# Second-layer products two channels at a time at every other half slot, in chunks 3 to 6 of a memory-attention and mixer kernel

## The chip, the cores and the metric

The kernel runs on one core of a Trainium2 chip. TensorE (PE) multiplies out of SBUF into PSUM, ScalarE (ACT), VectorE (DVE) and GpSimd (POOL) do the rest, SyncE (SP) issues most DMAs, and ACT issues some. Each engine takes its instructions in the order in which the program lists them. The metric is the device time of the whole kernel in microseconds, median of several runs.

## The reference

Two parts follow each other. The first is an attention through a memory of 32 slots for each of 8 x 8 heads over 576 tokens; the second a mixer over tokens and then over channels:

```python
a = softmax(phi, axis=tokens);  k_m, v_m = a^T k, a^T v
x = softmax(scale * q k_m^T) v_m               # heads side by side: 8 x 576 x 512
u = x + (relu(x^T w_tok1) w_tok2)^T            # token mixer
out = u + relu(u w_ch1) w_ch2                  # channel mixer, 512 -> 1536 -> 512
```

All of it is float32. The kernel splits a float32 operand into a high and a low part and multiplies three times (high by high, high by low, low by high) where this matters.

## The kernel before

The channel mixer works on 9 chunks of 512 tokens. Chunks 0 to 2 are computed straight. Chunks 3 to 6 (class `Quarters`, from `WIN` = 3 to `DOUBLE` = 7) take the first layer by a scheme of seven products of quarters in place of eight; chunks 7 and 8 do this jointly (class `Double`). Beside the mixer of one chunk runs the attention of the batches that later chunks need, laid out by hand in half slots: `at(h, fn)` files a piece of attention work under a half slot, `run(h, ...)` issues it there.

The change lies in `quarters(c, p)`, one step of chunk c for one pair p of hidden pieces: 4 chunks of 6 steps, 24 steps. A step issues seven first-layer products, named 11, 21, T2, T1, T3, 22 and T4, each six matmuls of 256 columns (L335). They go to two PSUM banks, `a` (rows "qa") and `b` (rows "qb"): 11, T2, T3 and T4 to a; 21, T1 and 22 to b. A product that adds onto its bank (T2, T3, 22, T4) or writes it anew (T1) has to wait until the result before it has been read out of that bank, most often by an ACT copy, `out`, L2166. The next step's two products take the same two banks.

Between the products stands the second layer: `mix` takes from `todo` one output channel block of one hidden piece of the step before and issues its three matmuls of 512 columns into an accumulator bank (L197, `Chunk.second`). `todo` holds eight such triples in a step (two hidden pieces by four channel blocks), and in the first step of chunk 3 four. `point(x)` stands behind each product, and once more at the end: first the attention work of that half slot, then a triple. The attention work on PE is `step_s` and `step_kv` (L754, L655), `step_A` (L896), `step_R` (L915) and `step_u` (L936). On ACT and DVE it is a softmax (`S_max`, `S_sub`, `S_exp` on L776), casts (`a_pair` on L826, `v_pair` on L840) and copies out of the attention's own two PSUM banks.

`load_unit` on ACT's queue fetches the weights of the products three units ahead.

Of the kernel before, what the change touches and what calls it, by code (L numbers as in the profile page):

```python
# [27 lines left out]
def kernel(  # L28
# [109 lines left out]
    def relu_high(h, ps):  # L138
        nc.scalar.activation(out=h, in_=ps, func=AF.Relu)  # L139

    def relu_low(h, l, ps):
        nc.vector.scalar_tensor_tensor(  # L142
            out=l, in0=ps, scalar=0.0, in1=f32(h), op0=ALU.max, op1=ALU.subtract
        )
# [423 lines left out]
    def load_unit(n, eng=nc.scalar):  # L568
        m = n - 2 * NF * (DOUBLE - WIN + 1)
        if m >= 7 * NF // 4:  # L570
            return
        p, j = n // 4 % (NF // 2), n % 4
        t = sb.tile([P, 1024], F32R, tag="c1", name=f"unit{n}", bufs=NF)
        if m >= 0:
            units[n] = t.rearrange("p (o x m) -> p o x m", o=2, x=2)
            eng.dma_start(out=f32(t), in_=Sums2.to[:, m // (NF // 4), m % (NF // 4)])
            return
        units[n] = t.rearrange("p (o x a n) -> p o x a n", o=2, x=2, a=2)
        m = 512 if j == 3 else 1024
        nc.scalar.dma_start(out=f32(t)[:, :m], in_=sums[p].to[:, j, :m])  # L580
# [1516 lines left out]
    for p in range(NF // 2):  # L2097
        x, h = Sums2(p), 2 * NF * (WIN + min(p, 4)) + (8.5 if not p else (3.5, 1.5, 9.5)[max(p - 3, 0)])
# [23 lines left out]
    def run(h, *ks):  # L2122
        for k in ks:
            for fn, x in events.pop((h, k), ()):
                out = fn(*x)
                if callable(out):
                    out()
# [20 lines left out]
    def quarters(c, p):  # L2148
        ch, h, n = chunks[c], 2 * NF * c + 4 * p, 4 * ((c - WIN) * NF // 2 + p)
        todo = [(x, f, a) for x, f in before if f < x.end for a in range(NKK)]  # L2150
        before[:] = [(ch, 2 * p), (ch, 2 * p + 1)]
        (eh, el), (oh, ol) = ch.pieces(p)
        t0, t1 = slice(0, HW), slice(HW, CW)

        def mix(n=1):
            for x, f, a in todo[:n]:
                x.ch2(f, [a])
                if f == x.end - 1:
                    x.add(a)
            del todo[:n]  # L2160

        def tile(x):
            return pch.tile([P, CW], F32, tag="ch", name=f"{x}{p}" + ch.n, bufs=2)

        def out(to, ps):
            nc.scalar.copy(out=to, in_=ps[:, :HW])  # L2166

        def add(to, x, y):
            nc.vector.tensor_tensor(out=to, in0=x, in1=y, op=ALU.add)  # L2169

        def product(ps, k, name, first):
            if not k % 2:
                load_unit(n + k // 2 + AHEAD)
            ch.product(ps, units[n + k // 2][:, k % 2], name, first, name in ("21", "22", "T4"))

        if not whole:
            whole.append(sb.tile([P, 2, CW], F32, tag="c1", name="whole", bufs=NF))
        et, ot = whole[0][:, 0], whole[0][:, 1]

        def split_relu(h, l, x):  # L2180
            relu_high(h, x)
            relu_low(h, l, x)

        def point(x):
            run(h + x, -1, 0, 1)
            mix()

        a = tile("qa")
        product(a, 0, "11", True)
        out(et[:, t0], a)  # L2190
        point(0)
        b = tile("qb")
        product(b, 1, "21", True)
        out(ot[:, t0], b)
        add(et[:, t0], et[:, t0], ot[:, t0])
        point(0.5)
        product(a, 2, "T2", False)
        out(et[:, t1], a)
        split_relu(eh[:, t0], el[:, t0], et[:, t0])
        point(1)  # L2200
        product(b, 3, "T1", True)
        out(ot[:, t0], b)
        point(1.5)
        product(a, 4, "T3", False)
        out(ot[:, t1], a)
        add(ot[:, t1], ot[:, t0], ot[:, t1])
        point(2)
        product(b, 5, "22", False)
        add(et[:, t1], b[:, :HW], et[:, t1])
        split_relu(oh[:, t1], ol[:, t1], ot[:, t1])  # L2210
        point(2.5)
        product(a, 6, "T4", False)
        split_relu(eh[:, t1], el[:, t1], et[:, t1])
        split_relu(oh[:, t0], ol[:, t0], a[:, :HW])
        point(3)
        point(3.5)
# [203 lines left out]
```

## Time and profile before

| | us |
|---|---|
| median of 3 runs | 745.86 (745.27 to 747.5) |
| profiled execution, its own time | 745.9 |
| its span | 743.9 |
| PE busy | 735.6 (99%) |
| DVE busy | 494.4 (66%) |
| ACT busy | 343.5 (46%) |
| chunks 3 to 6, first to last product of L335 | 299.9 to 619 |

A busy PE in this profile is one whose matmuls overlap: a matmul's row is longer than the distance to the next one's start. In timelines it is therefore the starts that tell how fast PE goes. Where a start comes later than the distance of its neighbours would have it, PE waited. ACT, DVE and POOL rows have a measured end, start plus duration.

### The profile page before, as it was taken

Reading aid. Unit: us, or ns where it says so; the run is one execution under the profiler, and the core shown is the slowest. Engines: PE = TensorE matmul, PEld = TensorE weight load, DVE = VectorE, ACT = ScalarE, POOL = GpSimd, SP = SyncE. Lnnn points to the kernel's source line nnn. Section 1 sums busy time; section 2 is a strip of 40 time slices with the busy share of each in tenths; the row PEclk is TensorE's granted clock in tenths of the full one; section 3 lists DMA queues with packets and bytes.
Section 4 is the critical chain, followed back from the end, with each engine's and each line's share of the span. In section 5 each row is a group of like instructions: output and inputs, shape, how many; then the busy total and the mean of one; then the engine's idle time right before and its main releaser. Section 6 shows DMA issues by size and latency. Waiting matters only on the chain.

```text
span 743.9 us, 12846 instructions
## 1 busy us (share of the span) xinstructions
PE 735.6 (99%) x4889; PEld 627.1 (84%) x4889; DVE 494.4 (66%) x896; ACT 343.5 (46%) x742; POOL 71.7 (10%) x71
## 2 busy tenths in 40 slices
PE   8999999999999999999999999999999999999998
PEld 8678787787878888889898889888898998888887
DVE  4989873776657657767586738674766554655874
ACT  5789753242314243545363536363544553434431
POOL 1021014001122020110010101010101000000000
PEclk9999999999999999999999999999999999999999
DMA  8975530575924654869687877879567645676762
GB/s 345 415 255 159 217 106 1 148 246 157 280 60 124 204 151 126 283 208 316 198 236 284 242 265 221 292 218 319 171 203 239 213 141 180 255 252 207 273 216 86
DMA packets 98813, 158.33 MB, mean 213 GB/s; under 512 B 42208, under 2 KB 65632, under 8 KB 94304
## 3 DMA queue, kind: packets, MB, share of 16 engines
q1 hardware_dynamic: 80320, 98.92, 41.0%
q10 hardware_dynamic: 18432, 58.60, 23.8%
q8 instruction: 39, 0.64, 0.4%
q14 instruction: 22, 0.18, 0.1%
HBM read 121.57 MB, written 35.91 MB: 212 GB/s over the span
## 4 chain that ended last, share of the span: by engine, by line
PE 80%; DMA 6%; DVE 6%; SPq 3%; ACT 2%; POOL 1%; issue 1%; ACTq 0%; POOLq 0%; DVEq 0%
PE acc L197 24%; PE cp L174 10%; PE qa L335 7%; PE e L455 7%; PE u L936 6%; PE qb L335 5%; PE da L400 4%; PE db L400 3%; PE Ap L896 2%; DMA sums<-v 2%; SPq L716 1%; PE sp L754 1%; POOL a L827 1%; DMA kv<-in_kv_dram 1%; PE u L1618 1%; PE end L455 1%
## 5 line engine op out<-in xcount | busy, mean ns | idle before, releaser
L197 PE MATMUL acc<-qhh,c 128*128 128x512 f32 x256 | 98.9, 396 | 0.0
L197 PE MATMUL acc<-hh,c 128*128 128x512 f32 x288 | 96.6, 394 | 0.0
L335 PEld LDWEIGHTS qa<-xT,unit 128*128 128x128 f32 x432 | 60.7, 188 | 8.2 <-ACT whole L2166 2.3
L335 PEld LDWEIGHTS qb<-x,unit 128*128 128x128 f32 x432 | 60.9, 188 | 6.7 <-ACT whole L2166 0.6
L197 PEld LDWEIGHTS acc<-hh,c 128*128 128x128 f32 x288 | 54.1, 188 | 14.3 <-issue 3.2
L335 PE MATMUL qa<-xT,unit 128*128 128x256 f32 x432 | 63.1, 282 | 0.8 <-ACT whole L2166 0.8
L335 PE MATMUL qb<-x,unit 128*128 128x256 f32 x432 | 63.0, 281 | 0.0
L827 POOL TENSOR_TENSOR a<-aT,a 64x576 fp32r<-64x576 f32 x22 | 34.0, 1544 | 300.6 <-ACT a L826 299.8
L197 PE MATMUL acc<-hl,c 128*128 128x512 f32 x144 | 56.3, 391 | 0.0
L197 PEld LDWEIGHTS acc<-qhh,c 128*128 128x128 f32 x256 | 48.1, 188 | 9.5 <-issue 3.3
L2169 DVE TENSOR_TENSOR whole<-whole 128x256 f32<-128x256 f32 x48 | 25.5, 531 | 44.2 <-ACT whole L2166 44.2
L197 PE MATMUL acc<-qal,c 128*128 128x512 f32 x192 | 53.7, 394 | 0.0
L142 DVE SCALAR_TENSOR_TENSOR hl<-cp,hh 128x512 fp32r<-128x512 f32 x36 | 24.7, 687 | 41.5 <-ACT hh L139 41.4
L174 PE MATMUL cp<-uh,c1h 128*128 128x512 f32 x144 | 51.4, 397 | 0.0
L197 PE MATMUL acc<-qhl,c 128*128 128x512 f32 x128 | 50.6, 395 | 0.0
L174 PE MATMUL cp<-ul,c1h 128*128 128x512 f32 x144 | 50.3, 390 | 0.0
L174 PE MATMUL cp<-uh,c1l 128*128 128x512 f32 x144 | 50.3, 390 | 0.0
L2166 ACT COPY whole<-qa 128x256 f32<-128x256 f32 x72 | 26.8, 372 | 45.7 <-PE qa L335 41.8
L142 DVE SCALAR_TENSOR_TENSOR qhl<-whole,qhh 128x256 fp32r<-128x256 f32 x48 | 22.3, 464 | 24.3 <-ACT qhh L139 24.0
L197 PEld LDWEIGHTS acc<-qal,c 128*128 128x128 f32 x192 | 32.7, 189 | 3.5
L2166 ACT COPY whole<-qb 128x256 f32<-128x256 f32 x48 | 17.8, 370 | 35.6 <-PE qb L335 35.4
L174 PEld LDWEIGHTS cp<-uh,c1l 128*128 128x128 f32 x144 | 27.0, 188 | 5.7
(295 smaller groups left out, 1652.6 us busy)
## 6 DMA issues: line engine op xcount, KB each, us to landing
unit<-sums ACTq DMA_DIRECT2D x93, 512.0 KB, 4.2
kv<-in_kv_dram SPq DMA_DIRECT2D x12, 1280.0 KB, 9.1
rawc<-in_w_ch_dram SPq DMA_DIRECT2D x12, 1024.0 KB, 6.5
q<-in_q_dram SPq DMA_DIRECT2D x16, 576.0 KB, 6.3
unit<-sums SPq DMA_DIRECT2D x18, 512.0 KB, 4.8
unit<-sums ACTq DMA_DIRECT2D x30, 256.0 KB, 3.8
sums<-sums SPq DMA_DIRECT2D x12, 512.0 KB, 5.8
sums<-v SPq DMA_DIRECT2D x12, 512.0 KB, 7.0
```

The costliest lines, as they stand in the source:

```text
L142: nc.vector.scalar_tensor_tensor(out=l, in0=ps, scalar=0.0, in1=f32(h), op0=ALU.max, op1=ALU.subtract)
L174: nc.tensor.matmul(ps, l[:, a, w], r[:, a], start=n == 0, stop=n == len(mm) - 1)
L197: nc.tensor.matmul(ps, l_[f // 2][:, f % 2, a * P : (a + 1) * P], r[:, w], start=f == start and x == 0, stop=f == end - 1 and x == 2,)
L335: nc.tensor.matmul(ps[:, :HW], l, r, start=first and n == 0, stop=n == len(mm) - 1, skip_group_check=not first,)
L400: nc.tensor.matmul(ps, l, r, start=first and n == 0, stop=n == len(mm) - 1, skip_group_check=not first,)
L455: nc.tensor.matmul(ps, weights[:, x, m], r[:, w], start=first and n == 0, stop=last and n == 2, skip_group_check=name in ("T2", "T3", "22"),)
L716: nc.sync.dma_start(out=s.kb[64 * hf : 64 * hf + 64], in_=s.keys)
L827: s.low_eng.tensor_tensor(out=l, in0=s.aT[own], in1=f32(h), op=ALU.subtract)
L896: nc.tensor.matmul(ps[:, :TT], a, w, start=x == 0, stop=x == len(mm) - 1)
L936: nc.tensor.matmul(ps[:, :HALF], a, r, start=x == 0, stop=x == len(mm) - 1)
L2166: nc.scalar.copy(out=to, in_=ps[:, :HW])
L2169: nc.vector.tensor_tensor(out=to, in0=x, in1=y, op=ALU.add)
```

## The change

`point(x)` issues no triple at the whole half slots (x = 0, 1, 2, 3) and two at the others (x = 0.5, 1.5, 2.5, 3.5). So two products stand back to back, 11 and 21, T2 and T1, T3 and 22, and two triples behind each such pair. T4 has two triples behind it as before.

```diff
         def point(x):
             run(h + x, -1, 0, 1)
-            mix()
+            if 2 * x % 2:
+                mix(2)
```

`mix(n)` issues the first n entries of `todo`. Nothing is added or removed: the same instructions are issued, with the same operands. ACT's list of instructions is the same row for row; DVE's differs in where the adds of finished accumulators (L215) stand; PE's differs throughout the 24 steps.

PE in step 1 of chunk 4, from T3 to T4. qa and qb are the two banks, acc0 to acc3 the accumulators of the channel blocks, unit30 and unit31 weights. Before:

```order
L335 MATMUL qa1_4_4193<-xT3_4_3940,unit30_4154 128x256 [waits DMAHW6_49,Activation_49]
L335 MATMUL qa1_4_4193<-xT3_4_3940,unit30_4154 128x256 x5
L197 MATMUL acc0_4_4256<-qhh01_4_4025,c20_521 128x512
L197 MATMUL acc0_4_4256<-qhl11_4_4026,c20_521 128x512
L197 MATMUL acc0_4_4256<-qhh01_4_4025,c20_521 128x512
L335 MATMUL qb1_4_4260<-x22_4_4012,unit30_4154 128x256 [waits Activation_49]
L335 MATMUL qb1_4_4260<-x22_4_4012,unit30_4154 128x256 x5
L197 MATMUL acc1_4_4283<-qhh01_4_4025,c20_521 128x512
L197 MATMUL acc1_4_4283<-qhl11_4_4026,c20_521 128x512
L197 MATMUL acc1_4_4283<-qhh01_4_4025,c20_521 128x512
L335 MATMUL qa1_4_4193<-xT4_4_4018,unit31_4194 128x256 [waits DMAHW7_49,Activation_49]
```

And with the change:

```order
L335 MATMUL qa1_4_4193<-xT3_4_3940,unit30_4154 128x256 [waits DMAHW6_49,Activation_49]
L335 MATMUL qa1_4_4193<-xT3_4_3940,unit30_4154 128x256 x5
L335 MATMUL qb1_4_4256<-x22_4_4012,unit30_4154 128x256 [waits Activation_49]
L335 MATMUL qb1_4_4256<-x22_4_4012,unit30_4154 128x256 x5
L197 MATMUL acc0_4_4279<-qhh01_4_4025,c20_521 128x512
L197 MATMUL acc0_4_4279<-qhl11_4_4026,c20_521 128x512
L197 MATMUL acc0_4_4279<-qhh01_4_4025,c20_521 128x512
L197 MATMUL acc1_4_4283<-qhh01_4_4025,c20_521 128x512
L197 MATMUL acc1_4_4283<-qhl11_4_4026,c20_521 128x512
L197 MATMUL acc1_4_4283<-qhh01_4_4025,c20_521 128x512
L335 MATMUL qa1_4_4193<-xT4_4_4015,unit31_4194 128x256 [waits DMAHW7_49,Activation_49]
```

The product 22 moved ahead of one triple; T3 and T4 have the same work ahead of them as before.

PE in step 3 of chunk 3, from 11 to the attention product R, whose inputs Ah and Al come from ACT and DVE. Before:

```order
L335 MATMUL qa3_3_3559<-x_3_2649,unit12_3435 128x256 [waits DMAHW1_49]
L335 MATMUL qa3_3_3559<-x_3_2649,unit12_3435 128x256 x5
L197 MATMUL acc0_3_3256<-qhh04_3_3386,c24_793 128x512 [waits Activation_49]
L197 MATMUL acc0_3_3256<-qhl14_3_3387,c24_793 128x512 [waits DVE_49]
L197 MATMUL acc0_3_3256<-qhh04_3_3386,c24_793 128x512
L335 MATMUL qb3_3_3574<-x21_3_2945,unit12_3435 128x256 [waits DVE_49]
L335 MATMUL qb3_3_3574<-x21_3_2945,unit12_3435 128x256 x5
L915 MATMUL Rp_4_1_3583<-vh_4_1_3158,Ah_4_1_3547 128x256 [waits Activation_49]
L915 MATMUL Rp_4_1_3583<-vl_4_1_3182,Ah_4_1_3547 128x256
L915 MATMUL Rp_4_1_3583<-vh_4_1_3158,Al_4_1_3548 128x256 [waits DVE_49]
```

And with the change:

```order
L335 MATMUL qa3_3_3559<-x_3_2649,unit12_3435 128x256 [waits DMAHW0_49]
L335 MATMUL qa3_3_3559<-x_3_2649,unit12_3435 128x256 x5
L335 MATMUL qb3_3_3571<-x21_3_2945,unit12_3435 128x256 [waits DVE_49]
L335 MATMUL qb3_3_3571<-x21_3_2945,unit12_3435 128x256 x5
L915 MATMUL Rp_4_1_3580<-vh_4_1_3158,Ah_4_1_3544 128x256 [waits Activation_49]
L915 MATMUL Rp_4_1_3580<-vl_4_1_3182,Ah_4_1_3544 128x256
L915 MATMUL Rp_4_1_3580<-vh_4_1_3158,Al_4_1_3545 128x256 [waits DVE_49]
```

21 and R moved ahead of the triple that stood between 11 and 21.

## Rows read from the trace of the kernel before

**Rows 1.** The page, busy time of an engine, its share of the span, and its instructions.

```profile
PE 735.6 (99%) x4889; PEld 627.1 (84%) x4889; DVE 494.4 (66%) x896; ACT 343.5 (46%) x742; POOL 71.7 (10%) x71
```

**Rows 2.** Who waited for whom, PE alone, from 299 to 622 us: us in total, times, longest.

```profile
PE qa L335 <- ACT whole L2166: 0.8, 1, 0.8
PE sp L655 <- ACT rest L957: 0.5, 2, 0.4
```

**Rows 3.** Timeline of PE in step 4 of chunk 5, a place where nothing waits: the product T1 in bank b, the first matmul of the triple behind it, and the product T3 in bank a. Columns of all timelines: start us, duration us, engine, line, what.

```profile
525.62 0.86 PE L335 MATMUL qb<-x,unit 128*128 128x256 f32 x6
526.33 0.39 PE L197 MATMUL acc<-qhh,c 128*128 128x512 f32 x1
...
527.02 0.87 PE L335 MATMUL qa<-xT,unit 128*128 128x256 f32 x6
```

**Rows 4.** Timelines of ACT, DVE and PE in step 1 of chunk 4, in order of time: the copy of T2 out of bank a, a relu of its sums, the low half of it on DVE, the softmax's exponentials, the copy of T1 out of bank b, and the product 22 in bank b.

```profile
402.69 0.37 ACT L2166 COPY whole<-qa 128x256 f32<-128x256 f32 x1 [1.00 <-PE qa L335]
402.96 0.42 ACT L139 ACTIVATE qal<-whole 128x256 fp32r<-128x256 f32 x1
403.41 0.42 DVE L142 SCALAR_TENSOR_TENSOR qal<-whole,qal 128x256 fp32r<-128x256 f32 x1 [0.97 <-ACT qal L139]
404.54 0.69 ACT L776 ACTIVATE S<-S 128x576 f32<-128x576 f32 x1 [1.16 <-DVE S L771]
405.13 0.35 ACT L2166 COPY whole<-qb 128x256 f32<-128x256 f32 x1
406.00 0.87 PE L335 MATMUL qb<-x,unit 128*128 128x256 f32 x6
```

**Rows 5.** Timelines of ACT and PE at the first and the last of six such places (step 4 of chunks 3, 4 and 5, step 1 of chunks 4, 5 and 6): the copy of T1 and the product 22.

```profile
364.84 0.35 ACT L2166 COPY whole<-qb 128x256 f32<-128x256 f32 x1
365.69 0.51 PE L335 MATMUL qb<-x,unit 128*128 128x256 f32 x3
...
567.20 0.36 ACT L2166 COPY whole<-qb 128x256 f32<-128x256 f32 x1
568.07 0.52 PE L335 MATMUL qb<-x,unit 128*128 128x256 f32 x3
```

**Rows 6.** Timelines of ACT and PE in step 5 of chunk 4: the first cast of the attention's rows, the cast `vv` that waits for POOL, the copy of T1, and the product 22.

```profile
451.67 0.67 ACT L826 CAST a<-aT 64x576 fp32r<-64x576 f32 x1
...
455.51 0.61 ACT L840 CAST vv<-vh 64x128 fp32r<-64x128 f32 x2 [0.49 <-POOL a L827]
...
456.67 0.37 ACT L2166 COPY whole<-qb 128x256 f32<-128x256 f32 x1
...
457.47 0.87 PE L335 MATMUL qb<-x,unit 128*128 128x256 f32 x6
```

**Rows 7.** The same two rows, copy of T1 and product 22, at the first and the last of four such places (step 2 of chunk 3, step 5 of chunks 3, 4 and 5).

```profile
334.85 0.37 ACT L2166 COPY whole<-qb 128x256 f32<-128x256 f32 x1
335.65 0.52 PE L335 MATMUL qb<-x,unit 128*128 128x256 f32 x3
...
538.16 0.37 ACT L2166 COPY whole<-qb 128x256 f32<-128x256 f32 x1
538.95 0.87 PE L335 MATMUL qb<-x,unit 128*128 128x256 f32 x6
```

**Rows 8.** Timelines of ACT and PE in step 2 of chunk 4: the copy of T1, the product 22 and the product T4; and the product 22 in step 2 of chunk 5.

```profile
416.17 0.37 ACT L2166 COPY whole<-qb 128x256 f32<-128x256 f32 x1
416.58 0.98 PE L335 MATMUL qb<-x,unit 128*128 128x256 f32 x6
418.13 0.98 PE L335 MATMUL qa<-xT,unit 128*128 128x256 f32 x6
...
497.86 0.98 PE L335 MATMUL qb<-x,unit 128*128 128x256 f32 x6
```

**Rows 9.** Timelines of DVE and PE in step 3 of chunk 3: the last read of the bank that 21 writes, the low half of A that R multiplies, the first matmul of R, and T2.

```profile
341.50 0.41 DVE L142 SCALAR_TENSOR_TENSOR qal<-qa,qal 128x256 fp32r<-128x256 f32 x1
342.43 0.41 DVE L136 TENSOR_TENSOR Al<-Ap,Ah 128x256 fp32r<-128x256 f32 x1
342.97 0.28 PE L915 MATMUL Rp<-vh,Ah 128*128 128x256 f32 x1
344.38 0.87 PE L335 MATMUL qa<-xT,unit 128*128 128x256 f32 x6
```

**Rows 10.** Timelines of PE and ACT at the other places where PE waits: the last matmul of a triple and T3 behind it in step 3 of chunk 3; sp in step 4 of chunk 4 and again of chunk 5, with the ACT row ahead of the latter; two pairs of matmuls of A in step 3 of chunk 5.

```profile
346.96 0.39 PE L197 MATMUL acc<-qhh,c 128*128 128x512 f32 x1
347.36 0.95 PE L335 MATMUL qa<-xT,unit 128*128 128x256 f32 x6
...
437.59 1.31 PE L655 MATMUL sp<-kv,phi 128*32 128x129 f32 x40 [0.17 <-ACT rest L957]
...
503.26 0.40 PE L896 MATMUL Ap<-w1h,nat 128*128 128x256 f32 x2
503.62 0.52 PE L896 MATMUL Ap<-w1h,nat 128*128 128x256 f32 x2
...
518.05 0.42 ACT L139 ACTIVATE qhh<-whole 128x256 fp32r<-128x256 f32 x1 [4.46 <-DMA sums<-v]
519.08 1.31 PE L655 MATMUL sp<-kv,phi 128*32 128x129 f32 x40 [0.36 <-ACT rest L957]
```

## The prediction, made before the changed kernel was run

> **What bounds the kernel now.** I read the page's busy times first: PE is busy 99% of the span, ACT and DVE about half [rows 1]. Such a share leaves open whether PE waits inside a stretch, so next came the waits of PE from 299 to 622 us, which hold all 24 steps: two entries, 1.3 us in all [rows 2]. Then the timeline, by the starts of PE's matmuls. Where nothing waits, a product takes 0.71 us (525.62 to 526.33) and a triple 0.69 (526.33 to 527.02) [rows 3]. So chunks 3 to 6 are a gapless stream on PE: reordering it can save little more than those 1.3 us, and the question is which results are now wanted earlier than they are ready. For that I set, at every product of the 24 steps, its start beside the end of the last read of its bank.
>
> **The change part by part.**
>
> *Matmuls.* None is added or removed; what PE itself does costs the same.
>
> *What moves.* Products 11, T2, T3 and T4 (bank a) have the same work ahead of them as before. Products 21, T1 and 22 (bank b), and attention work filed under half slots x.5, lose one triple ahead of them: they are due 0.70 us earlier. The triples at whole half slots go behind them, which for their inputs is only easier. Between two products of bank b the distance is the same as before; so a copy out of b has as much time as before if it follows PE. It has 0.70 us less where ACT or DVE comes to it late for another reason, since ACT's list is unchanged and its copies out of bank a stand between and do not come earlier. PE executes its list in order, so a b product that waits holds up everything behind it. The size of a new wait is then 0.70, less the distance from the copy's end to the product's old start, plus the hand-over. The hand-over is 0.04 to 0.05: the copy ended at 416.54 and 22 started at 416.58 [rows 8]. A product that had to wait also runs longer, 0.98 against 0.87 [rows 4, 8], so 0.11 goes on top.
>
> *Softmax places (six).* In step 1 of chunk 4 the copy of T1 ends at 405.13 + 0.35 = 405.48 and 22 starts at 406.00, 0.52 later [rows 4]. Ahead of that copy ACT does the exponentials (404.54), which wait for DVE; DVE had first to make the low half at 403.41, which waits for the relu at 402.96, which on ACT follows the copy of T2 at 402.69; and T2 is not moved. So this copy stays where it is. The distance is 365.69 - 365.19 = 0.50 at the first of the six and 568.07 - 567.56 = 0.51 at the last [rows 5]. New wait: 0.70 - 0.51 + 0.05 + 0.11 = 0.35 each, 2.1 us.
>
> *POOL places (four).* The copy of T1 stands behind the cast `vv`, and that waits for POOL, whose work began behind the cast at 451.67, close behind a copy out of bank a; 22 comes 457.47 - 457.04 = 0.43 behind the copy's end [rows 6], and 0.43 and 0.42 at the first and last of the four [rows 7]. New wait: 0.70 - 0.43 + 0.05 + 0.11 = 0.43 each, 1.7 us.
>
> *Two POOL places that wait already.* In step 2 of chunks 4 and 5 product 22 has waited for its copy and taken 0.98 [rows 8]. It cannot start earlier at all, and the whole 0.70 would be lost; but one step ahead lies a softmax place, whose 0.35 makes PE late without making this chain of DVE, POOL and ACT late. That leaves 0.35, less the 0.11 that T4 (0.98, row at 418.13) then no longer pays: 0.24 each, 0.5 us. The like place in chunk 6 has more room and gets nothing.
>
> *Step 3 of chunk 3.* R needs the low half of A, ready at 342.43 + 0.41 = 342.84, and started at 342.97 [rows 9]. It is now due 0.70 earlier, but PE comes 0.43 late from step 2, so it is due at 342.70 and starts at 342.89; with the longer first group 0.3 us. Behind it T2 (344.38) is late by as much.
>
> Gross: 2.1 + 1.7 + 0.5 + 0.3 = 4.6 us.
>
> *Given back.* A late PE finds some old waits over. sp waited 0.17 and 0.36 us in step 4 of chunks 4 and 5, after ACT had been held 4.46 us by a DMA (ACT went on at 518.05) [rows 10]. T3 came 0.40 behind the last matmul of its triple where 0.23 is usual (527.02 less 526.33, by three) and took 0.95: 0.25 [rows 3, 10]. Two pairs of matmuls of A took 0.52 against 0.40, in each of chunks 4 and 5: 0.24 [rows 10]. If none of these releases follows PE, 0.53 + 0.25 + 0.24 = 1.0 us comes back; if all do, nothing does. I take the whole 1.0, since the longest one is put down to a DMA.
>
> Net 4.6 - 1.0 = 3.6 us. The profiled execution took 745.9 us, the median 745.86; so 745.9 + 3.6 = 749.5 us. Own range: without the 0.11 per wait (about 11 waits, 1.2 us) 748.3; with nothing given back and the chains of step 2 moving along with PE (0.35 more at two places) 751.2.
>
> **A rule against it.** The copies' ends in rows 4 to 7 lie 0.42 to 0.52 us ahead of the products, in a stream that alternates two banks. The Trainium skill, Perfetto Trace Analysis, section "Optimizing Tensor Performance", says that independent groups of matmuls should rotate through PSUM banks, so that the evacuation of one overlaps the matmuls of the next. The change does just that, 11 and then 21 in the other bank at once, and by the rule alone nothing would be lost: 745.9 us. Here the trace disagrees in part: both banks are taken up again within the step, and it is the copy's place on ACT that decides, not the rotation.
>
> **Rivals.**
>
> *The chains come forward (not slower).* Product 21, its copy and the DVE add behind it come 0.70 us earlier, and with them the softmax's maximum, the subtraction and the exponentials; the POOL work likewise, if it depends more on the second cast, which follows the copy of 21, than on the first. Place: the exponentials and `vv` ahead of the copy of T1 [rows 4, 6]. From 0.28 us of advance on (0.70 - 0.43 + 0.01) no new wait is left, and the two old waits of rows 8 (0.15 each with their longer groups) go as well: 745.9 - 0.3 = 745.6; with both old waits of rows 2 gone too, 744.3. For it: DVE sat idle 0.97 us ahead of the low half [rows 4], so there is room. Against it: it idled for a relu that stands behind the copy of T2, and T2 cannot come earlier.
>
> *Nothing comes back, and more is late.* The DMA-held stretch of ACT and the casts follow PE, so that each new wait delays its own next chain. Then the gross sum stands, with step 2 at 0.35 more in two places and chunk 6's POOL place at its full 0.30: 745.9 + 4.6 + 0.7 + 0.3 = 751.5 us. For it: the first cast of the POOL chain follows a copy out of bank a, whose product follows PE. Against it: the longest of the old waits is put down to a DMA, and the copy of T1 in step 2 ends as late as it does for POOL's sake, not PE's.
>
> **How the numbers follow.** What this kernel's measurement can tell from no change is about 0.3%, 2.2 us: under 743.6 is faster, over 748.1 slower. The forecast, 749.5, has 0.58; its lower part, where the longer groups cost nothing and more comes back, falls within 0.3% with 0.07 of that. The chains that come forward have 0.26, 0.23 of it within 0.3% and 0.03 faster. The third case has 0.16, all slower. So slower 0.51 + 0.16 = 0.67, same 0.30, faster 0.03. The forecast's own range is 748.3 to 751.2; the range for 8 in 10 reaches down into the rival, to its 745.6, and up to 751.2.
>
> **What would show it.** In the profile after, the waits of PE from 299 to 622 us must list qb on ACT `whole` about ten times with 0.2 to 0.3 us each; 22 must stand 0.05 us behind the copy of T1 at the places of rows 5 and 7, and take 0.98. The copy of T1 must keep its distance of 2.4 us from the copy of T2 (405.13 less 402.69). If that distance has shrunk by 0.3, the first rival is right. sp in rows 10 without its wait shows the giving back. The prediction is wrong altogether if the 24 steps are longer with no such waits, or if PE's triples or products keep another pace than 0.69 and 0.71.

## The result, and the profile after

| | before | after |
|---|---|---|
| median, us | 747.43 (13 runs, 745.27 to 752.31) | 752.49 (13 runs, 750.04 to 758.13) |
| ratio to before | | 1.0077, interval 1.0057 to 1.0098 |
| profiled execution, its span | 745.9, 743.9 | 758.1, 756.1 |

The change makes the kernel slower, by more than was forecast. Two things make the numbers awkward. The profile of before shows one of its shortest executions and the profile of after its longest, so that the two traces differ by 12 us and the medians by 5. And single executions of before lie up to 10 us apart over all series (744.5 to 755.2 us); what the traces show of this stands below.

The page of after, busy times, answers to [rows 1]; the waits of PE in the 24 steps, us in total, times, longest, to [rows 2]:

```profile
PE 741.3 (98%) x4889; PEld 630.6 (83%) x4889; DVE 493.5 (65%) x896; ACT 344.0 (45%) x742; POOL 71.6 (9%) x71
```

```profile
PE Ap L896 <- ACT nat L135: 2.7, 1, 2.7
PE Ap L896 <- DVE nat L136: 2.0, 4, 0.8
PE qa L335 <- ACT whole L2166: 0.8, 1, 0.8
PE sp L655 <- ACT rest L957: 0.6, 1, 0.6
PE qb L335 <- ACT whole L2166: 0.4, 2, 0.2
```

The waits foreseen for qb are there twice, not ten times, and the largest entry is another: A, which waits for `nat`. But this view overlooks short waits. A place of [rows 4], step 1 of chunk 4, in ACT's timeline (the copy of T2, the exponentials, the copy of T1) and PE's (T3, 22, the triple behind):

```profile
410.77 0.37 ACT L2166 COPY whole<-qa 128x256 f32<-128x256 f32 x1 [1.70 <-PE qa L335]
...
412.62 0.69 ACT L776 ACTIVATE S<-S 128x576 f32<-128x576 f32 x1 [1.16 <-DVE S L771]
...
413.21 0.35 ACT L2166 COPY whole<-qb 128x256 f32<-128x256 f32 x1
```

```profile
412.68 0.87 PE L335 MATMUL qa<-xT,unit 128*128 128x256 f32 x6
413.61 0.98 PE L335 MATMUL qb<-x,unit 128*128 128x256 f32 x6
414.43 0.40 PE L197 MATMUL acc<-qhh,c 128*128 128x512 f32 x1
```

The copy of T1 still comes 2.44 us behind the copy of T2 and ends at 413.56; 22 starts 0.05 behind it. By starts, T3 takes 0.93 and 22 takes 0.82 where 0.71 is the pace [rows 3]: 0.33 us lost, with no wait printed, since T3's modelled end (413.55) hides it. The POOL place of [rows 6], ACT (the cast `vv`, the copy of T1) and PE (T3, 22, the triple):

```profile
465.51 0.61 ACT L840 CAST vv<-vh 64x128 fp32r<-64x128 f32 x2 [0.47 <-POOL a L827]
...
466.68 0.36 ACT L2166 COPY whole<-qb 128x256 f32<-128x256 f32 x1
```

```profile
466.07 0.87 PE L335 MATMUL qa<-xT,unit 128*128 128x256 f32 x6
467.09 0.98 PE L335 MATMUL qb<-x,unit 128*128 128x256 f32 x6
467.91 0.40 PE L197 MATMUL acc<-qhh,c 128*128 128x512 f32 x1
```

Again 22 starts 0.05 behind the copy; 1.02 and 0.82 in place of 0.71 make 0.42 us. The length of a step, from its first product to the next step's, after less before, at the forecast's places: softmax places 0.37, 0.14, 0.59 (step 4 of chunks 3, 4, 5) and 0.35, 0.35, 0.34 (step 1 of chunks 4, 5, 6); POOL places of step 5 0.41, 0.43, 0.41; the two that waited already 0.22, 0.21; the one in chunk 6 that was to get nothing 0.07. All steps but three sum to 3.6 us.

The three are step 2 of chunk 3 (12.24 us before, 17.60 after), step 0 of chunk 4 (+1.92) and step 3 of chunk 4 (+1.23). In the first, SP's queue of before and then of after (S sent out as rows in four pieces, then read back as `raw`):

```profile
327.92 2.88 SPq L851 DMA_DIRECT2D rows<-S  x4
332.71 0.38 SPq L858 DMA_DIRECT2D raw<-rows  x1
```

```profile
328.16 3.55 SPq L851 DMA_DIRECT2D rows<-S  x4
335.54 0.38 SPq L858 DMA_DIRECT2D raw<-rows  x1
```

ACT in after (the weight load, then the cast that waits for `raw`), and PE by windows (us, busy and rows, granted clock, DMA share, GB/s):

```profile
330.65 0.33 ACTq L580 DMA_DIRECT2D unit<-sums  x1
...
340.60 0.62 ACT L135 CAST nat<-raw 128x512 fp32r<-128x512 f32 x1 [3.58 <-DMA raw<-rows]
```

```profile
337.70:341.20 3.50, 0.90 (x7) 1.00 0.94 266
341.20:344.00 2.80, 2.50 (x14) 0.80 1.02 301
344.00:347.00 3.00, 3.00 (x13) 0.62 0.97 328
347.00:350.00 3.00, 3.00 (x22) 1.00 1.03 402
```

`raw` waits for the rows: it is issued 7.4 us after their first issue, before 4.8. And its read, of 256 KB, takes longer too: it lands 5.0 us behind its issue, before 3.3. Over the seven steps in which S goes out as rows, the reads' time to landing in the view of L858, before and then after:

```profile
DMA to landing us min/median/max: 2.9/3.4/4.4
DMA to landing us min/median/max: 2.8/4.6/5.0
```

PE stands still for 2.6 us of the first window, and then the granted clock falls: a mean of 0.80 and 0.62 in the two windows behind, a mix of its two levels, 2.4 and 1.2 GHz; from 347 it is 1.00 again. So a stop of 2.6 us and what came behind it, with this step's own late copy (0.42 by starts), made the step 5.4 us longer. How much of this belongs to the change is another matter, as a second profile of before will show. In the other two steps A waits for `nat` as well: the `raw` of the step before landed 11.2 and 10.8 us behind that step's first product, in before 7.9 and 8.3.

### The profile page after: what moved, and what is told of

The parts are those of the page before. It is cut to its first block, busy times and chain, and to the rows that moved or that the text cites. A ratio compares the mean times of both kernels' runs of the same rounds, so it can differ in the third digit from the quotient of the medians.

```text
span 756.1 us, 12848 instructions
## 1 busy us (share of the span) xinstructions
PE 741.3 (98%) x4889; PEld 630.6 (83%) x4889; DVE 493.5 (65%) x896; ACT 344.0 (45%) x742; POOL 71.6 (9%) x71
## 4 chain that ended last, share of the span: by engine, by line
PE 79%; DMA 7%; DVE 5%; ACT 3%; POOL 2%; issue 2%; SPq 1%; ACTq 0%; POOLq 0%; DVEq 0%
PE acc L197 23%; PE cp L174 10%; PE qa L335 7%; PE e L455 6%; PE u L936 6%; PE qb L335 5%; PE da L400 4%; PE db L400 3%; PE Ap L896 3%; DMA raw<-rows 2%; POOL a L827 2%; DMA rows<-S 1%; PE Rp L915 1%; PE sp L754 1%; DMA kv<-in_kv_dram 1%
## 5 line engine op out<-in xcount | busy, mean ns | idle before, releaser
L197 PE MATMUL acc<-qhh,c 128*128 128x512 f32 x256 | 91.1, 395 | 0.0
L335 PE MATMUL qb<-x,unit 128*128 128x256 f32 x432 | 65.5, 287 | 1.4 <-ACT whole L2166 0.4
L335 PEld LDWEIGHTS qb<-x,unit 128*128 128x128 f32 x432 | 56.5, 191 | 7.1 <-ACT whole L2166 3.8
L2169 DVE TENSOR_TENSOR whole<-whole 128x256 f32<-128x256 f32 x48 | 28.2, 587 | 37.8 <-ACT whole L2166 37.8
L197 PE MATMUL acc<-qal,c 128*128 128x512 f32 x192 | 49.7, 393 | 0.0
L197 PEld LDWEIGHTS acc<-qal,c 128*128 128x128 f32 x192 | 34.3, 188 | 5.7
L139 ACT ACTIVATE hh<-cp 128x512 fp32r<-128x512 f32 x36 | 21.4, 594 | 24.1 <-PE cp L174 24.1
```

Source lines behind the costliest of these rows:

```text
L197: nc.tensor.matmul(ps, l_[f // 2][:, f % 2, a * P : (a + 1) * P], r[:, w], start=f == start and x == 0, stop=f == end - 1 and x == 2,)
L335: nc.tensor.matmul(ps[:, :HW], l, r, start=first and n == 0, stop=n == len(mm) - 1, skip_group_check=not first,)
```

## The experiments

Times of before in one series are shared by its kernels. A ratio is the recorded estimate and not the quotient of two medians; the two differ by up to 0.002 (in the run that moves 21 alone with the late load: 1.0010, medians 749.23 and 747.33). "The rows steps" are the seven in which S goes out as rows; "the 13 steps" those in which the copy of T1 came late (softmax and POOL places).

**The change once more.**

> The changed kernel once more, for a second profile of it. Theory W (the waits of the prediction: products 22 of bank b behind late ACT copies) gives 3.6 us, a ratio of 1.005 to the kernel before, and in the profile some ten steps longer by 0.2 to 0.43 us. Theory D adds to W that the product 21, coming 0.7 us earlier, lets ACT issue a 512 KB load of weights 0.5 us earlier beside the DMAs that write the softmax's rows to DRAM; these then land 3 to 4.5 us behind the last issue instead of 2.4, the rows come back late, and A waits for them: 1.5 to 2.5 us more, a ratio of 1.007 to 1.008. In D the first profile's three long steps (5.4, 1.9 and 1.2 us more) are an extreme of the same, and here their sum is 1 to 4 us.

Measured: 751.28 us, ratio 1.0057 (1.0034 to 1.0080), and in the trace the same two kinds of loss: 0.35 and 0.43 us at the late copies, and 5.28 us in step 2 of chunk 3. The ratio lies between the two theories, nearer to W; the three long steps sum to 6.4 us (5.28, 0.01 and 1.13), where D expected 1 to 4. Over both series the kernel after has a median of 751.72 (25 runs).

**Only 21 moved, in the rows steps.**

```diff
         def point(x):
             run(h + x, -1, 0, 1)
-            mix()
+            rows = (c, p) in ((3, 2), (3, 5), (4, 2), (4, 5), (5, 2), (5, 5), (6, 2))
+            if not rows or x > 0.5:
+                mix()
+            elif x:
+                mix(2)
```

> The kernel before, with only the first pair moved (11 and 21 back to back, two triples behind) and only in the seven steps in which the softmax's rows go out to DRAM. W: no wait belongs to these moves, 0 us, ratio 1.000. D: the whole DMA part, 1 to 2.5 us, ratio 1.0015 to 1.0035; the rows land 3 us or more behind the last issue, and A waits for nat.

Measured: 753.47 us (7 runs), 1.0092 (1.0056 to 1.0128), beyond both expectations: seven moved products cost as much as the whole change, with no late copy anywhere. SP and ACT in step 5 of chunk 3, whose first product starts at 373.45:

```profile
373.18 2.27 SPq L851 DMA_DIRECT2D rows<-S  x4
379.78 0.38 SPq L858 DMA_DIRECT2D raw<-rows  x1
```

```profile
375.19 0.33 ACTq L580 DMA_DIRECT2D unit<-sums  x1
```

ACT issues a weight load of 512 KB (L580) as soon as the copy of the product ahead of it is under way. 21 is the product ahead, so the load goes out up to 0.7 us earlier, while the last rows (72 KB a piece) are being sent.

**Only 22 moved, in the 13 steps.**

```diff
-            mix()
+            late = (c, p) in (
+                (3, 2), (3, 4), (3, 5), (4, 1), (4, 2), (4, 4), (4, 5), (5, 1), (5, 2), (5, 4), (5, 5), (6, 1), (6, 2)
+            )
+            if not late or x not in (2, 2.5):
+                mix()
+            elif x > 2:
+                mix(2)
```

> The kernel before, with only the third pair moved (T3 and 22 back to back) and only in the 13 steps where the copy of T1 is late. W: nearly its whole sum, 3.0 to 3.8 us, ratio 1.004 to 1.005, each wait 0.2 to 0.3 and a longer group of 0.98. D alone, without W: 0 us. The rows' DMAs keep their 2.4 us.

Measured: 751.97 us, 1.0049 (1.0026 to 1.0072), that is 3.7 us. Nine of the steps with late copies are longer by 0.36, 0.42, 0.34, 0.23, 0.43, 0.33, 0.22, 0.40 and 0.34 us; step 2 of chunk 6, where nothing was due, by 0.01; the other three also hold waits for `nat` or sp that come and go. In step 2 of chunk 3 the rows do not keep their 2.4 us: `raw` is issued 6.9 us behind the first product, although the load is in its old place. So the late copies alone have the size that the forecast gave them.

**Pairs at the whole half slots**: 21 with T2, T1 with T3, 22 with T4.

```diff
         def point(x):
             run(h + x, -1, 0, 1)
-            mix()
+            if not 2 * x % 2:
+                mix(2)
```

> The changed kernel with the two triples at the whole half slots in place of the others: pairs 21 and T2, T1 and T3, 22 and T4. Bank a's products keep their place, bank b's come 0.7 us later than before. W: no new wait at 22, and the two old waits of 0.26 each go: -0.5 us, ratio 0.999 to 1.000. D: the load of weights is issued 0.7 us later, so the rows land no later than before: also 0 or below. A rival for which two triples or two products in a row cost by themselves: 3 us or more, as in the changed kernel.

Measured: 753.94 us (6 runs), 1.0085 (1.0055 to 1.0115), so the hope to gain fell. The rival's size is met, but the waits show another cause. The two largest waits of PE:

```profile
PE qa L335 <- ACT whole L2166: 4.0, 8, 0.9
PE sp L655 <- ACT rest L957: 2.6, 1, 2.6
```

Now bank a is wanted before ACT has copied it. The rows are back in 2.0 to 3.0 us here: a later 21 lets them pass.

**The weight load later, the products as in the kernel after.**

```diff
+        rows = (c, p) in ((3, 2), (3, 5), (4, 2), (4, 5), (5, 2), (5, 5), (6, 2))
...
-            if not k % 2:
+            if not k % 2 and (k != 2 or not rows):
                 load_unit(n + k // 2 + AHEAD)
...
         out(et[:, t1], a)
+        if rows:
+            load_unit(n + 1 + AHEAD)
```

> The kernel after, but in the seven steps that send S out as rows (L851) the weight load that ACT issued ahead of its copy of T2 is issued behind that copy. Nothing on TensorE is moved. Theory (two costs: ACT's late copies, about 3.6 us, and a weight load that ACT issues too early beside the rows): the load now starts 1 us or more behind the last rows, the rows are back within 1.9 to 2.6 us of the last issue as in the kernel before, TensorE no longer waits for nat beyond some 0.5 us, and the ratio to the kernel before falls from about 1.0065 to 1.003 to 1.005. Rival (the rows come late for another reason, the weight load has no part in it): rows still 3 to 4.5 us, ratio 1.006 to 1.008.

Measured: 751.90 us, 1.0063 (1.0040 to 1.0086). The rows did what was expected (back in 2.2 to 3.1 us), the time did not fall: a miss for the theory that the early load costs the kernel after much in most of its executions. But A still waits for `nat`, beyond the expected 0.5 us:

```profile
PE Ap L896 <- DVE nat L136: 1.0, 2, 0.7
```

In step 2 of chunk 4 `raw` was issued in time, 5.1 us behind the first product, and landed only 5.7 us later (2.9 in before); step 3 is 1.21 us longer than in before. So the late load is no clean removal of the early one: the rows are sent sooner, and their read takes longer.

**Only T1 moved, in all 24 steps.**

```diff
             run(h + x, -1, 0, 1)
-            mix()
+            if x != 1:
+                mix(1 + (x == 1.5))
```

> The kernel before, with only the second pair of products brought together (T1 directly behind T2, the channel between them moved behind T1) in all 24 steps; 21 and 22 keep their places. Theory: this pair meets neither a late copy nor the rows, so the ratio is 0.999 to 1.001 and no wait of TensorE is added. Rival (two products one behind the other cost time in themselves, wherever they stand): one third of the loss of the kernel after, 1.002 to 1.003.

Measured: 747.93 us, 1.0019 (0.9998 to 1.0040): its estimate lies between the two theories, and neither is excluded.

**Late load, and the planned work behind T1.** The load is moved as in the run above; the rest of the edit:

```diff
-        point(1)
+        if not late:
+            point(1)
         product(b, 3, "T1", True)
         out(ot[:, t0], b)
+        if late:
+            point(1)
```

> The kernel after with two things undone without moving the products apart: the weight load behind the copy of T2 in the seven rows steps (as in the run beside it), and in the 13 steps in which the copy of T1 came late the work planned for that half slot is issued behind T1 and its copy, in place of ahead of them. Theory: the copy of T1 then stands ahead of the exponentials and the value casts on ACT, TensorE's waits of 0.2 to 0.3 us ahead of 22 and the slowed 22 go, and with the rows back in time the ratio is 0.999 to 1.001. Rival (the softmax or the token work, 0.7 us later, is now what is late): ratio 1.003 to 1.006 with waits for S, a or nat in their place.

Measured: 749.00 us, 1.0029 (1.0011 to 1.0048). Step 1 of chunk 4, ACT (the copy of T1, the exponentials) and PE (T3, 22, the triple):

```profile
405.58 0.37 ACT L2170 COPY whole<-qb 128x256 f32<-128x256 f32 x1
406.66 0.68 ACT L776 ACTIVATE S<-S 128x576 f32<-128x576 f32 x1 [0.70 <-DVE S L771]
```

```profile
406.72 0.88 PE L335 MATMUL qa<-xT,unit 128*128 128x256 f32 x6
407.43 0.88 PE L335 MATMUL qb<-x,unit 128*128 128x256 f32 x6
408.15 0.40 PE L197 MATMUL acc<-qhh,c 128*128 128x512 f32 x1
```

The copy now stands ahead of the exponentials, 22 follows T3 after 0.71 and takes 0.72: the loss of 0.33 is gone. In its series the ratio fell from 1.0063 to 1.0029, 2.5 us; the two intervals just overlap. What is left was to be nothing and is about 2 us, at the edge of the rival's 1.003 to 1.006, and the waits for `nat` that the rival named are there: 3.5 us in this execution.

**The kernel before once more, one execution.**

> The kernel before once more, for a second profile of it. Theory (the profile that the forecast rested on was one of its fastest): a span of 745 to 750 us, with rows back within 2 to 3 us, and some us of waits for nat or for the copies of rest on ACT that the first profile did not have. Rival (the first profile was typical): span within 1 us of 743.9 and the same waits.

Measured: 755.8 us, a span of 753.7, beyond what either expectation allowed. Its two largest waits of PE in the 24 steps, ACT in step 4 of chunk 4, and PE by windows behind it:

```profile
PE sp L655 <- ACT rest L957: 3.2, 1, 3.2
PE Ap L896 <- ACT nat L135: 2.2, 1, 2.2
```

```profile
443.75 0.33 ACTq L580 DMA_DIRECT2D unit<-sums  x1
444.12 0.42 ACT L139 ACTIVATE qhh<-whole 128x256 fp32r<-128x256 f32 x1 [7.34 <-DMA sums<-v]
```

```profile
445.10:448.60 3.50, 3.45 (x56) 0.50 0.74 255
448.60:451.20 2.60, 2.60 (x17) 0.51 0.00 1
451.20:455.00 3.80, 3.80 (x28) 1.00 0.34 92
```

The kernel before has these waits too: ACT held at a weight load until a store landed (7.34 us, in the first profile 4.26 and 4.46), sp late by 3.2, then the lower clock for 6 us; with the late rows (step 2 of chunk 3, 16.71 us) 10 us in all. The first profile had neither loss. So step 2 of chunk 3, the longest difference between the profiles of before and after, is no work of the change alone.

**Work behind T1, loads as in the kernel after.** The edit is that of the run with the late load and the planned work behind T1, without its change to the load.

> The kernel after with the planned work of that half slot behind T1 and its copy in the 13 steps (as in e7_behind), but with the weight loads where the kernel after has them. Theory (two costs that hide each other: the waits for the late copies, 3.6 us, also give the rows time, so that the early weight load costs little beside them): without the copies' waits the early weight load costs more than it did in the kernel after, as when 21 alone was moved; rows come back late (raw issued 5.6 to 6.4 us after a step's first product) and the ratio is 1.004 to 1.009, above the 1.0029 of e7_behind. Rival (the two add up, and the weight load's part is 1 us or less): 1.002 to 1.004.

Measured: 749.80 us, 1.0028 (1.0000 to 1.0056). `raw` is issued 5.6 to 6.2 us behind the first product in six of the seven steps, as expected, yet PE waits for `nat` only 0.6 us in this execution: the reads are short here, 2.7 to 3.1 us, so that `raw` lands at 9.0 us at the latest, where the kernel after has up to 11.7. The rival (it adds up, and the load has a small part) had the number.

**Only 21 moved, with the late load.** Order of products as in the run that moved 21 alone; the load as above.

> The kernel in which only 21 was moved in the seven rows steps (1.0092), with the weight load behind the copy of T2 there; the order of the products is the same. Theory (the early weight load beside the rows is the whole of that loss): raw is issued 4.0 to 5.1 us after a step's first product in place of 5.7 to 6.5, and the ratio falls to 0.999 to 1.002. Rival (the move of 21 itself costs, by its copies on ACT or the sums on DVE): it stays at 1.006 or more.

Measured: 749.23 us, 1.0010 (0.9988 to 1.0032), against 1.0092. SP and ACT in the same step, whose first product starts at 371.71:

```profile
371.44 2.34 SPq L851 DMA_DIRECT2D rows<-S  x4
376.26 0.38 SPq L858 DMA_DIRECT2D raw<-rows  x1
```

```profile
375.52 0.33 ACTq L580 DMA_DIRECT2D unit<-sums  x1
```

The load goes out 2.1 us later in the step, and `raw` is issued 1.8 us sooner. The intervals don't touch: here the early load was the loss.

**The kernel before with the late load.**

> The kernel before with only the weight load of T2 issued behind the copy of T2 in the seven rows steps. Theory (the same contest of DMAs costs the kernel before something too, in most of its executions): raw is issued earlier in step 2 of chunk 3 (some 5 us behind the step's first product, where the second profile of before has 6.8), and the ratio is 0.996 to 0.999, less scattered. Rival (before has slack enough): 0.999 to 1.001.

Measured: 747.28 us, 0.9990 (0.9969 to 1.0012): no gain that can be told. Its profile is like the first of before: `raw` issued 4.2 to 5.6 us behind the first product, 1.4 us of waits in the 24 steps.

**The change without the guilty pairs.**

```diff
-            mix()
+            rows = (c, p) in ((3, 2), (3, 5), (4, 2), (4, 5), (5, 2), (5, 5), (6, 2))
+            late = rows or (c, p) in ((3, 4), (4, 1), (4, 4), (5, 1), (5, 4), (6, 1))
+            keep = (0, 0.5) * rows + (2, 2.5) * late
+            if x in keep or x > 2.5:
+                mix()
+            elif 2 * x % 2:
+                mix(2)
```

> The kernel after without the pairs that the runs so far hold guilty: in the seven rows steps 21 keeps its place, in the 13 steps with a late copy 22 keeps its place; all other pairs are made (21 behind 11 in 17 steps, T1 behind T2 in all 24, 22 behind T3 in 11). Theory (the late copies and the early weight load are the whole loss): no wait of TensorE for whole ahead of qb, raw issued at 4.2 to 5.5 us as in the kernel before, ratio 0.999 to 1.0015. Rival (something else in the pairs costs 1 to 2 us too): ratio 1.002 to 1.004, as in the two kernels that took the late copies' waits away.

Measured: 748.42 us, 1.0009 (0.9988 to 1.0029). PE's waits in the 24 steps:

```profile
PE Ap L896 <- ACT nat L135: 2.0, 1, 2.0
PE sp L655 <- ACT rest L957: 1.4, 1, 1.4
PE qa L335 <- ACT whole L2166: 0.8, 1, 0.8
PE Ap L896 <- DVE nat L136: 0.2, 1, 0.2
```

None is for bank b, and these are waits that before has too, in one or the other of its two profiles. `raw` is issued 6.5 us behind the first product in step 2 of chunk 3, later than expected, at 4.1 to 5.5 in the other six steps. The 52 pairs that are left cost nothing that can be told, though the interval reaches into the rival's 1.002 to 1.004.

**What the rows did, side by side.** From a rows step's first product to the issue of `raw`, us, in the order of the seven steps, read from SP's and PE's timelines; when ACT issued the weight load, behind the same product; and how long `raw`'s read then took to land, least, median and most, from the view of L858:

| kernel | raw issued | load | read |
|---|---|---|---|
| before | 4.1, 4.4, 5.5, 4.2, 4.3, 4.5, 4.4 | 2.4 to 2.5 | 2.9, 3.4, 4.4 |
| before, second profile | 6.8, 4.4, 5.4, 4.4, 4.5, 4.3, 4.2 | 2.4 to 2.5 | 2.8, 3.8, 4.7 |
| after | 6.7, 6.4, 6.2, 4.2, 4.8, 4.9, 4.2 | 1.7 to 1.8 | 2.8, 4.6, 5.0 |
| after once more | 6.6, 6.1, 6.2, 5.6, 4.3, 5.7, 5.3 | 1.7 to 1.8 | 2.7, 3.2, 5.1 |
| 21 alone | 6.5, 6.3, 5.8, 6.3, 4.2, 6.4, 5.7 | 1.7 to 2.2 | 2.9, 4.6, 5.3 |
| work behind T1 | 6.2, 6.1, 5.6, 5.7, 5.6, 6.1, 4.3 | 1.7 to 1.9 | 2.7, 2.8, 3.1 |
| 21 alone, late load | 4.5, 4.6, 5.4, 4.7, 4.6, 4.3, 4.3 | 3.8 to 4.3 | 4.0, 4.4, 5.7 |
| after, late load | 4.9, 4.3, 5.1, 4.2, 4.4, 4.3, 4.0 | 3.8 to 3.9 | 3.9, 4.6, 5.7 |

A needs the landing, not the issue, and the last column shows two things. Where `raw` went out late enough to meet ACT's next weight load (6.1 to 6.6 us behind the first product in most steps), its read took 4.5 to 5.3 us. And the late load, which lands 7.4 to 9.2 us behind the first product, runs beside the read: in step 2 of chunk 4 of the three kernels with 21 moved and the late load, `raw` landed 10.8 to 11.5 us behind the first product, and the next step was 1.2 to 2.3 us longer.

Step 2 of chunk 3 is a case by itself. The load was left in its place in the second profile of before and in the runs that moved 22 alone, T1 alone, or all but the guilty pairs; there too `raw` went out at 6.5 to 7.1 us in these four profiles, and the step was 2.9 to 4.5 us longer than in the first profile of before. Step 0 of chunk 4 speaks for the early load: it was longer by 1.92 us in the kernel after and 2.14 with 21 alone, and in no other profile by more than 0.17.

## Why the prediction was wrong

**The waits for the copies: right, place by place.** *Softmax places*: 0.35 each, measured 0.34 to 0.37 at four of the six (at the other two, 0.14 and 0.59, sp's old waits stand in the same step), with 0.05 from the copy's end to 22, 0.98 for 22, and 2.44 us between the two copies as before. *POOL places*: 0.43 each, measured 0.41 to 0.43 in step 5; the fourth lies in the long step 2 of chunk 3, where T3 and 22 by their starts lose 0.42. *Two that wait already*: 0.24, measured 0.22 and 0.21; chunk 6 0.07 where nothing was due. The net of 3.6 us is the sum of all steps but three, to the tenth in part by luck: this sum lacks the 0.42 of step 2 of chunk 3 and holds 0.24 of a longer sp wait. And 22 moved alone in the 13 steps cost 1.0049, 3.7 us. That these waits are the cause is shown from the other side too: with the copy ahead of the exponentials they are gone, and the ratio falls by 0.0034. The 52 pairs whose copies are in time cost nothing that can be told (1.0009); for them the rule of the Trainium skill, Perfetto Trace Analysis, section "Optimizing Tensor Performance", holds: with another bank for the next group, the evacuation overlaps. Where an engine in order comes late to the copy, 0.33 to 0.43 us were lost in spite of it.

**The terms beside them.** *Given back*: of the two waits of sp the first came back (step 4 of chunk 4 only 0.14 longer); the second did in the repeat (step 4 of chunk 5 shorter by 0.01) and not in the first profile (longer by 0.59). T3's wait in step 3 of chunk 3 came back: that step is 14.45 us long in place of 14.70. The slow pair of A came back in chunk 5 (step 3 is 0.11 shorter) and not in chunk 4, where A waits. That makes some 0.6 of the 1.0 in the first profile and 0.9 in the repeat. *Step 3 of chunk 3* (0.3 for R) does not show: in both profiles of the kernel after PE came to R over 5 us late. A fault of the way of proof: the waits view was to list qb ten times and lists it twice, since a matmul's modelled end reaches past a wait of 0.2 us.

**The step that failed: the base of the sum.** "The profiled execution took 745.9 us, the median 745.86; so 745.9 + 3.6": three runs were too few for a kernel that scatters from 744.5 to 755.2 us. In the series of the result 13 runs of before have 747.43, and 747.43 + 3.6 is 751.0, inside the range. The median after, 752.49, is 3.0 above the forecast: 1.5 of that is the base, 1.5 the change, which by the medians cost 5.1 there in place of 3.6. Over the 97 runs of before in the series of the experiments the median is 747.31; the 25 runs of after have 751.72, 2.2 above the forecast: 1.4 of that is the base, 0.8 the change.

**The step that was missing: what ACT's queue sends.** "What moves" says that 21 is due 0.70 earlier and follows this to the copies. It did not follow the weight load behind that copy, nor ask what runs beside it on the DMA engines. The load goes out 0.6 to 0.7 us earlier, while the rows of S are being sent; outside step 2 of chunk 3 `raw` is issued up to 2.0 us later and lands up to 3.3 us later; A waits, and behind a long wait the clock can fall. That this chain exists and can cost 6 us is shown by moving 21 alone, with the load early (1.0092) and late (1.0010). What it costs the kernel after is not shown: with the late load that kernel has 1.0063, without it 1.0067 on the mean of two series, but the late load has a price of its own, the longer read. So no run puts the 0.8 to 1.5 us that the change cost beyond the forecast down to this chain. In the rows steps the kernel after starts its first product some 0.35 us later against the rows (they go out 0.63 ahead of it, in the kernel with 21 alone 0.27 to 0.29), because the step before has just lost that much to a late copy; 22 moved alone gives the same 0.63. That this is why the two costs don't add up was argued and not shown: the run made for it (copies in time, load early) has 1.0028 and does not bear it out, nor does it settle it, since its rows still go out 0.57 ahead.

**What stays open.** The medians differ by 751.72 - 747.31 = 4.4 us, the copies' waits explain 3.6. Four kernels move 21 in the rows steps and have no late copy: 21 alone has 1.0092 and with the late load 1.0010; the work behind T1 has 1.0028 and with the late load 1.0029. Two that leave 21 in its place there have 1.0009 and 1.0019. So 1 to 2 us may belong to 21 and the rows behind it, but these intervals, 0.002 to 0.003 to either side, overlap, except that 21 alone lies above the others and touches that of the work behind T1; no run settles it. Why the early load cost 6 us with 21 alone and nothing that can be told with the work behind T1 stays open too: there the reads were short, and why is not shown.

**The rivals.** *The chains come forward* fell: the distance between the two copies did not shrink, and where the work was moved behind T1 by hand the waits went, which is what that rival would have needed. *Nothing comes back* fell by its mechanism, since old waits did come back; its 751.5 is near the measured time for another reason.

## What to carry to other kernels

When an instruction comes earlier, follow everything queued behind it on every engine that waits for it, the DMAs first, and each DMA to its landing: a load that starts half a microsecond earlier can cost more than the waits that were counted. Read short waits from the starts of matmuls, not from the list of waits. And before a forecast of a few microseconds, look at how far single executions of the kernel lie apart, because a profile shows one of them.

## What was not expected of the hardware

A long wait was paid nearly twice. Behind PE's stop of 2.6 us in the kernel after the granted clock had a mean of 0.80 and 0.62 over the next 5.8 us, and the step became 5.4 us longer, 0.42 of it the late copy; in the second profile of before 3.2 us of waiting and 6.1 us at 0.50 made a step 5.8 us longer (20.73 in place of 14.94). Near 2 us it can go either way: with 21 alone moved PE was idle for 1.8 us between 337 and 341, and the clock fell to 0.75 and 0.68 in the two windows behind; with 22 alone moved it was idle for 2.0 us there and kept 1.00. The executions' mean clock shows who is hit, a grouping made after the runs: it was 0.998 or less in 22 of 97 executions of before (median 750.2, the others 746.8) and in 7 of 25 of the kernel after (755.7, the others 751.3), but in only 2 of 46 of the four kernels with the late load. There the late load seems to help, in the long executions more than in the median.

The neighbour of a small transfer matters by fractions of a microsecond. From the end of the last issue of the four 72 KB pieces to the next issue that waits for them, in the six later rows steps: 2.2 to 2.4 us and once 3.4 before, where the 512 KB load starts 0.8 to 1.2 us behind the last piece's issue; 3.4 to 4.3 us and once 2.1 with 21 alone moved, where it starts 0.4 to 0.7 behind; 2.0 to 2.7 and once 3.3 with the late load. One case stands against a plain rule: with T1 alone moved the load started 0.9 behind the last piece in step 2 of chunk 4, and the rows still took 4.1.

The read of `raw` (256 KB) shows the same. In the ten profiles whose load is not late it took 4.5 to 5.3 us in all 15 cases in which it was issued 0.25 us or less ahead of ACT's next weight load, or behind it, and in the other 55 a median of 3.45 (2.7 to 4.6, once 5.3); this grouping too was made after the runs. In the four profiles with the late load it took 3.5 to 5.9.
